# Padding the on-chip buffers of a softcap attention + MLP kernel so that matmul operands start at other addresses modulo 256

## The chip, the cores and the metric

The kernel runs on one core of a Trainium2 chip. The metric is the device time of one execution in microseconds (us); the median over the runs of a version counts. Matmuls run on TensorE (PE in the profile, its weight loads PEld), elementwise work on VectorE (DVE), ScalarE (ACT) and GpSimd (POOL), and transfers are issued mostly by SyncE (SP). SBUF is the on-chip memory of 128 partitions; an address below is the byte offset inside a partition.

## What is computed

Attention with a soft cap over 4 batches, 12 heads, 448 positions and head size 64, then a two-layer MLP on its 1792 x 768 result, all in float32:

```python
scores = cap * np.tanh(scale * (q @ k.T) / cap)
attn = np.exp(scores - scores.max(-1)); attn = attn / (attn.sum(-1) + 1e-09)
x = (attn @ v)                      # heads side by side: 1792 x 768
h = x @ w_in                        # 768 x 2048
g = np.maximum(0.01 * h, h)
return g @ w_out                    # 2048 x 768
```

## The kernel before

The 24 pairs of heads (4 batches, 6 pairs each) are worked on one after the other. For a pair, the transposed keys and queries lie in SBUF, `scores` (L490 to L499) multiplies them into PSUM, ScalarE applies tanh and exp (L521, L523) into the tiles `pf`, `values` (L504) multiplies `pf` with the rows of v, and VectorE divides by the sums and writes a piece of x. The first 12 pairs use full float32 matmuls; from pair 12 on (`fs=12`), keys and queries are split into a high and a low part of type float32r, and three products stand for one.

The MLP runs over four stretches of the 1792 rows. The first stretch (256 rows) multiplies float32 tiles: weights from `ws`, columns from `bank_0` and three later banks (L673). The second (512 rows) splits weights and columns into high and low parts of type float32r, so that each product is three matmuls of 128 x 128 weights and 512 moving columns: high x high, high x low, low x high (L673). The third and fourth stretch are done together in a scheme with seven products of sums and differences of blocks (`plan_duo`, L895), followed by the second layer (`plan_last`, L992), again three float32r matmuls of 512 columns per product.

All weights of the float32r matmuls of the MLP lie in the four tiles `w_0` to `w_3`. The moving columns lie in many places: in `xh` and `xl` (the parts of x for the second stretch), in the eleven `bank_j` tiles (parts of the hidden layer), and, once attention is over, in the memory that held `raws`, `odd`, `exps`, `norm` and `heads_h` during attention, which `places` hands out in slots of 512 columns. The list is

```python
homes = xl_slots + places("raws") + places("heads_h") + places("odd") + places("exps") + places("norm") + bank_slots
```

Every tile is made by `tile_of` (L210), directly, through `ring`, or through `chunk` (one tile that holds several small ones), in a pool with one buffer per name. The pool lays the tiles one behind the other in the order in which they are made and rounds each size up to a multiple of 32 bytes. `life` makes a second, third or fourth tile under the tag of an old one and so reuses its address. All columns that a matmul picks out of a tile start a multiple of 256 bytes behind the tile's start (512 float32 columns are 2048 bytes, 448 are 1792, 128 are 512, 64 are 256). So a tile's start modulo 256 is also the start modulo 256 of every operand read from it.

The order of the work is set by `Plan.issue`, a planner with costs and due times written into the table `T`; it knows nothing of addresses.

Of the kernel before, what the change touches and what calls it, by code (L numbers as in the profile page):

```python
# [9 lines left out]
F32 = mybir.dt.float32  # L10
# [151 lines left out]
def softcap_attention_mlp(  # L162
# [14 lines left out]
    P = 128  # L177
# [29 lines left out]
    def f32(ap):  # L207
        return ap.bitcast(F32)

    def tile_of(name, shape, dt=F32, pool=const, tag=None):  # L210
        t = pool.tile(shape, dt, name=name, tag=tag or name)
        return t

    def ring(tag, n, shape, dt=F32, pool=const):
        plan.ring(tag, n)
        tiles[tag] = [tile_of(f"{tag}_{i}", shape, dt, pool) for i in range(n)]
# [9 lines left out]
    def chunk(name, *parts):  # L226

        size = sum(n * cols for _, n, cols, _ in parts)
        whole = tile_of(name, [P, size])
        chunks[name] = (size, [])  # L230
        rows, lo = {}, 0
        for tag, n, cols, view in parts:
            for i in range(n):
                ap = whole[:, lo:lo + cols]
                lo += cols
                rows.setdefault(tag, []).append(ap.rearrange(view[0], **view[1]) if view else ap)
                chunks[name][1].append((tag, i))
        return rows
# [48 lines left out]
    for tag in ("kT", "qT"):  # L287
        alias(tag, rows[tag + "0"] + rows[tag + "1"], [0 if parted_of(i) else i % 2 for i in range(n_pairs)])
    heads_h = tile_of("heads_h", [P, 2, S], F32R)
    for x, nm in enumerate("kq"):  # L290
        alias(nm + "h", [heads_h[:, x]])
# [864 lines left out]
```

## Time and profile before

| | us |
|---|---|
| median of 3 runs | 688.72 |
| lowest and highest of them | 687.26, 2277.24 |
| profiled execution, whole | 689.4 |
| profiled execution, span from first to last instruction | 687.6 |
| PE busy in the span | 653.6 |

The durations below are those of the profiled execution; 1.8 us of it lie outside the span. In the profile a matmul's end is modelled and overlaps the next matmul's start, so what one costs in a dense stream is read from the distance between starts: the start of the next row of the timeline minus the start of this one, divided by the number of matmuls in this one. A full float32 matmul stands as two records, a float32r matmul as one.

### The profile page before, as it was taken

The page shows a single profiled execution, that of the slowest core. Times are in us where ns is not written, and L with a number is a line of the kernel's source. Part 1 is how long each engine was busy: PE and PEld are TensorE (multiplying, and loading weights), DVE is VectorE, ACT ScalarE, POOL GpSimd, SP SyncE. Part 2 cuts the span into 40 slices and gives each one's busy share as a digit, 9 for nine tenths or more (in the row PEclk, how much of TensorE's full clock was granted, in tenths as well). Part 3 has the DMA queues.
Part 4 walks back from the last instruction along what each step waited for, and adds up shares of the span by engine and source line. Part 5 has one row for each costly group of instructions (what it writes and reads, how often), then busy time and mean ns, then how long its engine had stood idle before and what let it go on. Part 6 is the DMA issues. An engine that isn't in the chain of part 4 may idle for free.

```text
span 687.6 us, 8588 instructions
## 1 busy us (share of the span) xinstructions
PE 653.6 (95%) x2932; PEld 457.7 (67%) x2932; DVE 446.9 (65%) x693; ACT 367.7 (53%) x611; POOL 73.5 (11%) x87
## 2 busy tenths in 40 slices
PE   8878989999989899999999999999999899999995
PEld 4223455566666567878666878878788687888884
DVE  3739759887889997587687786864856881121210
ACT  5877959886879776484575353433424840110000
POOL 8111201000121020010310020000000200000000
PEclk9998999999999999999999999999999999999999
DMA  9888988998859877312233143310212213144212
GB/s 135 138 237 166 260 246 197 303 256 259 232 130 227 229 170 198 115 46 85 74 91 91 58 95 86 84 47 23 82 33 57 91 42 73 38 92 92 38 27 33
DMA packets 186308, 85.60 MB, mean 124 GB/s; under 512 B 148240, under 2 KB 172816, under 8 KB 186256
## 3 DMA queue, kind: packets, MB, share of 16 engines
q1 hardware_dynamic: 182576, 83.23, 49.0%
q0 software_dynamic: 768, 1.38, 1.1%
q10 hardware_dynamic: 2912, 0.36, 0.4%
q8 instruction: 25, 0.41, 0.3%
q14 instruction: 27, 0.22, 0.1%
HBM read 66.85 MB, written 18.09 MB: 124 GB/s over the span
## 4 chain that ended last, share of the span: by engine, by line
PE 77%; DVE 8%; ACT 6%; DMA 6%; issue 1%; SPq 1%; DVEq 0%; ACTq 0%
PE m L673 27%; PE sc L992 19%; PE sc L895 11%; PE po L504 7%; PE po L895 4%; PE sc L493 3%; DMA bank<-in_moe_w_in_dram 3%; PE m L895 2%; ACT exps L521 2%; PE sc L499 2%; DVE bank L626 1%; DVE ws L629 1%; ACT exps L523 1%; PE sc L490 1%; DMA scratch<-ws 1%
## 5 line engine op out<-in xcount | busy, mean ns | idle before, releaser
L258 ACT CAST w<-ws 128x384 fp32r<-128x384 f32 (+2 forms) x99 | 62.9, 654 | 133.8 <-PE sc L992 75.1
L265 DVE TENSOR_TENSOR w<-ws,w 128x384 fp32r<-128x384 f32 (+2 forms) x93 | 68.0, 744 | 74.8 <-ACT w L258 74.4
L673 PE MATMUL m<-bank,ws 128*128 128x256 f32 x384 | 92.7, 391 | 2.8 <-DVE ws L629 2.8
L673 PEld LDWEIGHTS m<-bank,ws 128*128 128x128 f32 x384 | 71.7, 192 | 28.6 <-DVE ws L629 8.1
L521 ACT ACTIVATE exps<-sc 128x896 f32<-128x896 f32 (+1 forms) x96 | 76.0, 819 | 27.2 <-PE sc L493 15.1
L504 PE MATMUL po<-exps,norm 128*64 128x448 f32 x384 | 79.5, 547 | 1.3 <-ACT exps L523 0.7
L523 ACT ACTIVATE exps<-exps 128x896 f32<-128x896 f32 (+1 forms) x96 | 79.8, 857 | 0.4
L673 PE MATMUL m<-bank,w 128*128 128x512 f32 x288 | 68.5, 392 | 0.0
L992 PE MATMUL sc<-bank,w 128*128 128x512 f32 x270 | 64.2, 390 | 0.0
L673 PEld LDWEIGHTS m<-bank,w 128*128 128x128 f32 x288 | 53.5, 188 | 12.8 <-issue 1.3
L673 PE MATMUL m<-xh,w 128*128 128x512 f32 x192 | 61.4, 393 | 0.0
L992 PEld LDWEIGHTS sc<-bank,w 128*128 128x128 f32 x270 | 50.7, 188 | 10.9
L504 PEld LDWEIGHTS po<-exps,norm 128*64 128x64 f32 x384 | 25.0, 136 | 45.7 <-issue 36.8
L673 PEld LDWEIGHTS m<-xh,w 128*128 128x128 f32 x192 | 36.0, 188 | 9.7 <-DVE w L265 0.7
L1005 DVE STREAM_TRANSPOSE ot<-sc 128x512 f32<-128x512 f32 x12 | 8.6, 717 | 49.0 <-PE sc L992 49.0
L673 PE MATMUL m<-xl,w 128*128 128x512 f32 x96 | 37.4, 390 | 0.0
L622 ACT ACTIVATE bank<-bank 128x768 int32<-128x768 uint8 (+1 forms) x34 | 29.8, 875 | 12.2 <-DMA bank<-in_moe_w_in_dram 9.9
L626 DVE SCALAR_TENSOR_TENSOR bank<-bank 128x768 int32<-128x768 int32 (+1 forms) x34 | 30.9, 913 | 3.5 <-ACT ws L624 3.4
L527 DVE TENSOR_TENSOR norm<-exps 128x896 f32<-128x896 f32 x23 | 24.9, 1083 | 11.3 <-ACT exps L523 6.6
L629 DVE SCALAR_TENSOR_TENSOR ws<-ws,bank 128x768 int32<-128x768 int32 (+1 forms) x34 | 31.6, 930 | 0.5
L530 POOL TENSOR_TENSOR norm<-norm,exps 64x448 f32<-64x448 f32 x12 | 14.9, 1239 | 154.9 <-ACT exps L523 95.2
L624 ACT ACTIVATE ws<-bank 128x768 f32<-128x768 f32 (+1 forms) x34 | 29.6, 874 | 0.2
(188 smaller groups left out, 1056.2 us busy)
## 6 DMA issues: line engine op xcount, KB each, us to landing
ws<-scratch SPq DMA_DIRECT2D x44, 384.0 KB, 3.1
bank<-in_moe_w_in_dram SPq DMA_DIRECT2D x16, 768.0 KB, 6.2
scratch<-ws SPq DMA_DIRECT2D x22, 384.0 KB, 4.2
bank<-in_moe_w_out_dram SPq DMA_DIRECT2D x12, 640.0 KB, 5.4
ws<-scratch SPq DMA_DIRECT2D x24, 320.0 KB, 2.9
raws<-in_k_dram SPq DMA_DIRECT2D x96, 56.0 KB, 3.9
norm<-in_v_dram SPq DMA_DIRECT2D x48, 96.0 KB, 4.1
bank<-in_moe_w_out_dram SPq DMA_DIRECT2D x6, 768.0 KB, 6.5
```

The source lines that it names most:

```text
L258: nc.scalar.copy(o, i)
L265: ENG[eng].tensor_tensor(out=o, in0=a, in1=f32(b), op=ALU.subtract)
L504: nc.tensor.matmul(at("po", 2 * i)[half[j], 0:S], at("vc", i)[:, c], pf(g)[:, j if wide(g) == 2 else 0], start=(g == 0), stop=(g == NG - 1))
L521: a = plan.add(r, {"act": ct}, lambda e, sc=sc, g=g: nc.scalar.activation(pf(g), sc(), AF.Tanh, scale=scale_of["tanh"]), vers("sc", [g]) + ...
L523: plan.add(r, {"act": ct + 0.03}, lambda e, g=g: nc.scalar.activation(pf(g), pf(g), AF.Exp, scale=scale_of["exp"]), (), vers("pf", [g]), a ...
L622: a = plan.add(rank, {"act": ca}, lambda e: nc.scalar.activation(word(0), top(), AF.Copy, bias=1.0 / 64 - 0.5, scale=1.0 / 32), [("wr", m) ...
L624: b = plan.add(rank, {"act": ca}, lambda e: nc.scalar.activation(ws(), word(1).bitcast(F32), AF.Abs, scale=2.0 ** -112), [("wr", m)], [("w ...
L626: a = plan.add(rank, {"dve": cv}, lambda e: nc.vector.scalar_tensor_tensor(out=word(1), in0=word(1), scalar=-0x80000000, in1=word(0), op0= ...
L629: plan.add(rank, {"dve": cv}, lambda e: nc.vector.scalar_tensor_tensor(out=z(), in0=z(), scalar=3, in1=word(1), op0=ALU.logical_shift_left ...
L673: nc.tensor.matmul(ps(), l, r, start=begins and some[0] == 0 and i == 0, stop=ends and some[-1] == len(cs) - 1 and i == len(ops) - 1)
L895: nc.tensor.matmul(ps(), l, r, start=start and x == 0, stop=x == len(ops) - 1, skip_group_check=not start)
L992: nc.tensor.matmul(ps(), l, rr, start=first and x == 0, stop=final and x == len(ops) - 1)
```

## The change

`tile_of` gets a table of nine names. Ahead of a tile whose name is in it, it makes one more tile of 8 float32 (32 bytes) times the number in the table, which nothing reads or writes. All tiles made later move up by the same amount.

```diff
+    PADS = {"raws": 1, "odd": 1, "exps": 1, "norm": 1, "heads_h": 1, "xh": 5, "xl": 1, "bank_0": 1, "w_0": 7}
+
     def tile_of(name, shape, dt=F32, pool=const, tag=None):
+        if PADS.get(name):
+            pool.tile([P, 8 * PADS[name]], F32, name=f"pad_{name}", tag=f"pad_{name}")
         t = pool.tile(shape, dt, name=name, tag=tag or name)
         return t
```

No instruction is added, removed or moved: on every engine the built program has the same rows in the same order, with the same semaphores waited for; only buffer numbers and addresses differ. The pads are 19 times 32 bytes, 608 in all, and the last tile now ends at byte 228864 of its partition instead of 228256. The start addresses in the two built programs, modulo 256, and the number of float32r matmuls of 512 columns that read their moving columns there (1656 in all; their weights are in `w` each time):

```
tile            before          after    moving 512-column matmuls
raws        16928 =  32     16960 =  64      112
odd         27680 =  32     27744 =  96       42
exps        32288 =  32     32384 = 128      210
norm        53792 =  32     53920 = 160      210
heads_h     75808 =  32     75968 = 192       14
xh          80288 = 160     80608 = 224      192
xl          92576 = 160     92928 =   0      222
bank_0     118688 = 160    119072 =  32      654 (all banks; each is 6144 = 24 x 256 bytes)
ws_0       194464 = 160    194848 =  32        -
w_0        203680 = 160    204288 =   0        weights of all 1656
```

So in the kernel before, 1068 of these matmuls (`bank`, `xl`, `xh`) move columns from the same address modulo 256 as their weights, and 588 (`raws`, `odd`, `exps`, `norm`, `heads_h`) from an address 128 bytes away from it. In the changed kernel the distance is 32 bytes for `bank`, 32 on the other side for `xh`, 0 for `xl`, 64 for `raws`, 96 for `odd`, 128 for `exps`, 96 on the other side for `norm` and 64 on the other side for `heads_h`. The float32 matmuls of the first stretch (`bank_0` and `ws`) keep the distance 0.

## Rows read from the trace of the kernel before

**Rows 1.** The page, busy time, share of the span and instructions of each engine.
```profile
PE 653.6 (95%) x2932; PEld 457.7 (67%) x2932; DVE 446.9 (65%) x693; ACT 367.7 (53%) x611; POOL 73.5 (11%) x87
```
**Rows 2.** The page, chain that ended last, share of the span by engine.
```profile
PE 77%; DVE 8%; ACT 6%; DMA 6%; issue 1%; SPq 1%; DVEq 0%; ACTq 0%
```
**Rows 3.** Busy time of each engine in stretches of the span.
```profile
core 0: us, PE busy (x) PEld busy (x) DVE busy (x) ACT busy (x) POOL busy (x), PEclk, DMA share, GB/s
...
43.00:240.00 197.00, 185.42 (x852) 108.18 (x852) 162.09 (x251) 158.78 (x256) 23.85 (x28) 0.97 0.89 232
...
254.00:400.00 146.00, 145.75 (x692) 107.32 (x692) 109.28 (x153) 85.28 (x141) 14.33 (x9) 1.00 0.34 92
400.00:577.00 177.00, 172.33 (x741) 137.51 (x737) 120.46 (x199) 75.66 (x144) 13.34 (x10) 1.00 0.24 65
577.00:687.60 110.60, 101.85 (x443) 82.69 (x441) 18.00 (x23) 8.36 (x11) 0.00 (x0) 0.99 0.28 56
```
**Rows 4.** Waits of PE from 250 to 687 us, longest of seven and the shortest.
```profile
PE sc L895 <- ACT bank L258: 1.4, 2, 0.7
PE sc L895 <- DVE xh L905: 1.2, 1, 1.2
...
PE po L551 <- DVE xh L581: 0.2, 1, 0.2
```
**Rows 5.** Timeline of PE, 651 to 674 us: start, us, operation, count.
```profile
651.30 6.31 PE L992 MATMUL sc<-bank,w 128*128 128x512 f32 x27
657.44 2.20 PE L992 MATMUL sc<-xl,w 128*128 128x512 f32 x9
659.48 1.79 PE L992 MATMUL sc<-raws,w 128*128 128x512 f32 x7
661.11 0.39 PE L992 MATMUL sc<-heads_h,w 128*128 128x512 f32 x1
661.34 0.40 PE L992 MATMUL sc<-raws,w 128*128 128x512 f32 x1
661.58 1.56 PE L992 MATMUL sc<-norm,w 128*128 128x512 f32 x6
...
668.45 2.26 PE L992 MATMUL sc<-norm,w 128*128 128x512 f32 x9
670.55 0.86 PE L992 MATMUL sc<-odd,w 128*128 128x512 f32 x3
671.25 2.27 PE L992 MATMUL sc<-exps,w 128*128 128x512 f32 x9
673.35 0.85 PE L992 MATMUL sc<-bank,w 128*128 128x512 f32 x3
```
**Rows 6.** Chain that ended last, in order of time: start, us, what.
```profile
118.79 2.59 PE m L673 x12
123.99 2.79 PE m L673 x12
```
**Rows 7.** Timeline of PE in attention, float32r scores of a pair.
```profile
246.17 0.37 PE L493 MATMUL sc<-heads_h,odd 64*128 64x448 f32 x2
246.38 0.37 PE L493 MATMUL sc<-heads_h 64*128 64x448 f32 x2
246.58 0.37 PE L493 MATMUL sc<-odd,heads_h 64*128 64x448 f32 x2
246.79 0.37 PE L493 MATMUL sc<-heads_h,odd 64*128 64x448 f32 x2
```
**Rows 8.** Line L258 on ACT: duration ns min/median/max, by tiles.
```profile
L258 ACT CAST bank<-bank x7: 614/622/635, 544.1 to 552.1; 128x512 fp32r<-128x512 f32 x7
...
L258 ACT CAST norm<-bank x5: 621/622/625, 537.1 to 539.2; 128x512 fp32r<-128x512 f32 x5
```
**Rows 9.** Line L265 on DVE: duration ns min/median/max, by tiles.
```profile
L265 DVE TENSOR_TENSOR bank<-wait,bank x6: 684/689/691, 426.4 to 562.8; 128x512 fp32r<-128x512 f32 x6
...
L265 DVE TENSOR_TENSOR exps<-bank,exps x5: 685/687/687, 550.6 to 560.4; 128x512 fp32r<-128x512 f32 x5
```
**Rows 10.** Issues of DMA: count, KB each, median us to landing.
```profile
raws<-in_k_dram SPq DMA_DIRECT2D x96, 56.0 KB, 3.9
```

## The prediction

> **What bounds the kernel now.** I read the page's busy shares first: TensorE is busy for 95% of the span [rows 1], and 77% of the chain that ended last is PE [rows 2]. A busy share of PE says little by itself, so the stretches come next [rows 3]. From 254 us on, PE is busy for 145.75 of 146, 172.33 of 177 and 101.85 of 110.6 us, while DVE and ACT have room (120.46 and 75.66 of 177) and the DMA engines are at 0.24 to 0.34. In these 433 us stand all 1656 float32r matmuls of 512 columns. The waits of PE from 250 us on come to under 6 us: seven rows, the longest 1.4 us [rows 4]. So there the time is the number of matmuls times the distance between their starts, and what a pad does to that distance goes into the end nearly one for one. Before 240 us attention and the first stretch of the MLP share the chip: PE 185.42 of 197 us, with ACT, DVE and DMA nearly as full [rows 3].
>
> The timeline then gives that distance by the tile that the columns come from [rows 5]. Nine matmuls on `xl` start at 657.44 and the next row at 659.48: 2.04 / 9 = 0.2267 us each. Twenty-seven on `bank`: (657.44 - 651.30) / 27 = 0.2274. The nine on `raws` and `heads_h` from 659.48 to 661.58: 0.2333; nine on `norm`, 668.45 to 670.55: 0.2333; nine on `exps`, 671.25 to 673.35: 0.2333. Same shape, same weight tiles, same stage, no wait between. What differs is the address: `xl` and `bank` start at 160 modulo 256 like their weights, the other four at 32, 128 bytes away. So start addresses cost 0.0067 us per matmul, and this trace has two points of the curve.
>
> A third row I take as the floor: twelve records of the float32 matmuls of 256 columns take 2.59 us, 0.2158 each [rows 6] (the 2.79 us run beside it begins after another kind of matmul). A record there has half the columns and takes nearly as long, so it must spend about twice the time on a column and need its operands at about half the rate. So 0.0109 us of the 0.2267 and 0.0175 of the 0.2333 lie above the floor, and reading operands out of SBUF is the likeliest owner.
>
> The Trainium skill, page "SBUF — State Buffer", section "Who interferes with whom", says that PE's read port for moving columns and its port for weights are independent and that PE never waits on anyone. By that the pads change nothing. The 0.2267 against 0.2333 speaks against it; it is a rival below.
>
> **The change part by part.** Nothing is added or moved on any engine, and no wait is new; the one thing to price is the distance between starts of each group of matmuls. I take the reading that the surcharge follows the distance between the moving columns and the weights modulo 256, since both streams are read at the same time. Known are distance 0 (0.2267) and 128 (0.2333). Distances 32, 64 and 96 are not in this trace. Their lower bound is the floor, 0.2158. Their upper bound is 0.24: the largest single distance in the rows, from 661.34 to 661.58, and as far above 0.2333 as that lies above 0.2267. Between ends this far apart I take 0.2300, midway between the two rows measured on this shape, because nothing says which of the two an in-between distance resembles.
>
> - `bank`, 654 matmuls, distance 0 to 32: 654 x (0.2300 - 0.2267) = +2.2 us.
> - `xh`, 192, distance 0 to 32 on the other side: +0.6 us.
> - `raws`, `odd`, `norm`, `heads_h`, together 378, distance 128 to 64 or 96: 378 x (0.2300 - 0.2333) = -1.2 us.
> - `xl`, 222, stays at 0 and `exps`, 210, at 128: nothing. Cover for that is the reading itself; under the second rival below they do change.
> - Scores of the last 12 pairs: each pair has 12 starts of 448 float32r columns about 0.207 us apart [rows 7]. In 8 of the 12 columns and weights now lie in `heads_h` and `odd`, 96 apart, where both stood at 32. 96 x 0.0033 x 448/512 = +0.3 us; bounds are -1.0 and +1.1 by the same two ends.
> - Float32 matmuls: `bank_0` with `ws` keeps distance 0. `values` goes from 0 to 32 (columns in `exps`, weights in `norm`). They need their operands at the half rate of the floor row [rows 6], so 0. If that cover were gone, 192 starts x 0.0067 = 1.3 us, in a stage where PE has 11.6 us of idle time in 197 to soak it up [rows 3]; and no less than 0, as they have nothing to lose.
> - ACT and DVE: the same cast takes 622 ns with its output at 160 or at 32 modulo 256 [rows 8], the two-input subtraction 689 and 687 [rows 9]. Priced at 0, bounded by those 2 ns x 700 instructions, 1.4 us to either side, beside other work.
> - DMA: every start stays a multiple of 32 bytes; only `raws` now begins on one of 64. Its 56 KB pieces land in 3.9 us [rows 10] and are issued pairs ahead. Priced at 0. Were they a tenth faster or slower, one first load, 0.4 us, would show at the start.
>
> Sum: 2.2 + 0.6 - 1.2 + 0.3 = +1.9 us on the profiled execution's 689.4, so 691.3. That execution is 0.7 above the median of the runs shown, 688.72; against that the forecast is 690.6. The bounds: at the floor all 1656 give 1068 x 0.0109 + 588 x 0.0175 = 21.9 us less, 667 against the median; at 0.24 the changed groups give 846 x 0.0133 + 378 x 0.0067 + 1.1 = 14.9 us more, 703.6.
>
> The Trainium skill, page "TensorE: Matmul & The Clock Gate", section "Back-to-back issue gap", gives a spacing of N / 2.4 + 2.5 ns for an isolated matmul, 215.8 ns at 512 columns. The floor above agrees (0.2158), the float32r rows do not; by the rule alone there would be 21.9 us to win, the low bound just given.
>
> **Rivals.**
>
> *Addresses do nothing.* The difference between the tiles would come from something that goes with them and not from their place. For it: both groups vary by some ns. Against it: six groups of tiles, split exactly by address, with the same weights. Time 688.7.
>
> *The moving address alone counts, not the weights'.* Then `bank` takes over the row of address 32: 654 x 0.0067 = +4.4. `norm` arrives at 160: 210 x -0.0067 = -1.4. `xl` and `xh`, 414, go to unknown addresses, midway: +1.4; `exps`, `raws`, `odd`, `heads_h`, 378, likewise: -1.2. Sum +3.2, so 691.9. For it: in this trace all weights of these matmuls sit at 160, so the two readings can't be told apart; the scores with both operands at 32 are about 0.207 apart, 0.018 above the floor of 0.2158 x 448/512 = 0.189, where distance 0 would give 0.0109 x 448/512 = 0.010 and address 32 would give 0.015. Against it: these come in short runs of pairs, and the first matmuls of a run are slower anyway.
>
> *Faster: the half-line rule.* All operands before start 32 bytes past a multiple of 64. If the surcharge is that of reading across such a border, then `xl`, `exps`, `raws` and `heads_h`, now with their weights on multiples of 64, fall to the floor: 222 x 0.0109 + 336 x 0.0175 = 8.3 us, so 680.4. If the weights' alignment alone decides, all 1656 do, 667. For it: the surcharge exists at distance 0 too. Against it: 32 and 160 are alike in this respect and yet cost different amounts, so it can't be the whole.
>
> *Slower: the two streams run into each other at 32 bytes.* Place: `bank` and `xh`, 846 matmuls, half of the whole. The two streams start a few ns apart, and a neighbour on either side could be met at each step where an equal start is met at few. A spacing of 0.2500, the same 0.0233 above 0.2267 that is a tenth of the matmul, costs 846 x 0.0233 = 19.7 us: 708.4. It decides from 0.2430 up, where 846 x 0.0163 = 13.8 us is 2% of the time. For it: most matmuls are moved from the cheapest distance known. Against it: 128 bytes away, the farthest from equal, costs just 0.0067.
>
> **How the numbers follow.** Forecast with its prices between the two rows: 0.55. Moving address alone: 0.20. Half-line rule for the four groups: 0.09; for all by the weights: 0.03. Streams that collide: 0.07. Nothing: 0.06. The likeliest case gives 690.6. The range 681 to 700 holds the forecast with `bank` and `xh` anywhere from 0.2187 (846 x 0.0080 = 6.8 us less, and 0.9 for the other terms) up to their bound of 0.24 (699.1), the second rival and no change; outside stay the half-line cases (0.12) and the collision (0.07). About 2% is what a measurement of this kernel can tell from no change, 13.8 us. Over 2% faster: the all-weights case and a little of the forecast's lower tail, 0.04. Over 2% slower: the collision and a little of the upper tail, 0.08. Within: 0.88.
>
> **What would show it right or wrong.** In the timeline of the changed kernel the runs on `xl` should again be 0.2267 apart and those on `exps` 0.2333 if distance counts; if the moving address alone counts, `norm` shows 0.2267 and `bank` 0.2333. `bank` is the row to read first: each 0.001 us on it is 0.65 us of the whole. The float32 runs should stay at 0.2158, the casts at 622 ns, and the waits of PE after 250 us under 6 us. The prediction is wrong if `bank` leaves 0.2187 to 0.24, or if the time moves while these distances do not.

## The result, and the profile after

The changed kernel takes 693.05 us (median of 6 runs, 689.97 to 694.52), the kernel before 688.11 (6 runs beside it): a ratio of 1.0069 with a 95% interval of 1.0041 to 1.0096. It is slower, by about 4.9 us, and by less than 2%. One of the six executions of the kernel before took 2277.24 us; the ratio leaves it out, and the median without it is 687.50. The profiled execution spans 690.9 us against 687.6.

The split of the span at the 1004th matmul record, which is the same place in both programs, says where. The first view is busy time by stretches of the kernel before, the second of the changed kernel.

```profile
0.00:243.00 243.00, 222.69 (x1004) 123.10 (x1004) 189.33 (x302) 190.20 (x305) 41.23 (x63) 0.98 0.89 215
243.00:687.60 444.60, 430.93 (x1931) 334.57 (x1928) 257.60 (x392) 177.53 (x307) 32.26 (x24) 1.00 0.30 75
```
```profile
0.00:242.00 242.00, 219.99 (x1004) 121.78 (x1004) 189.53 (x302) 190.32 (x305) 41.74 (x64) 1.00 0.89 216
242.00:690.90 448.90, 435.72 (x1930) 334.56 (x1928) 257.74 (x392) 177.39 (x307) 32.31 (x24) 0.99 0.29 74
```

The part with the float32r matmuls grew from 444.6 to 448.9 us, 4.3 more, and PE's busy time with it (4.8). DVE, ACT and POOL are busy as long as before. The clock is not the difference: from 240 to 680 us the granted clock is 1.00 in every stretch of 20 us of both traces. The first part is 1.0 us shorter in this pair of executions. Nothing should be read into that: in the five experiments below that have every tile of attention at 160, the 1005th matmul record starts anywhere between 241.5 and 243.4 us.

The timeline of PE in the changed kernel, for the same stretch as [rows 5] (start, us, operation, count; the distance between starts is the next row's start minus this one's, over the count):

```profile
654.43 6.46 PE L996 MATMUL sc<-bank,w 128*128 128x512 f32 x27
660.73 2.23 PE L996 MATMUL sc<-xl,w 128*128 128x512 f32 x9
662.79 1.78 PE L996 MATMUL sc<-raws,w 128*128 128x512 f32 x7
664.41 0.39 PE L996 MATMUL sc<-heads_h,w 128*128 128x512 f32 x1
664.64 0.40 PE L996 MATMUL sc<-raws,w 128*128 128x512 f32 x1
664.88 1.57 PE L996 MATMUL sc<-norm,w 128*128 128x512 f32 x6
...
671.89 2.25 PE L996 MATMUL sc<-norm,w 128*128 128x512 f32 x9
673.98 0.86 PE L996 MATMUL sc<-odd,w 128*128 128x512 f32 x3
674.68 2.26 PE L996 MATMUL sc<-exps,w 128*128 128x512 f32 x9
676.78 0.40 PE L996 MATMUL sc<-bank,w 128*128 128x512 f32 x1
```

`bank` went from 0.2274 to 6.30 / 27 = 0.2333. `xl` went from 0.2267 to 0.2289, `raws` with `heads_h` from 0.2333 to 0.2322, `norm` from 0.2333 to 0.2322; `exps` stayed at 0.2333. The starts are printed to 0.01 us, so over nine matmuls 0.0011 is one step of the print. The merged chain shows the same over longer stretches, here its rows of 108 matmuls on `xh` and `xl` and of the last 441, before and after:

```profile
267.19 24.70 PE m L673 x108
...
578.07 101.59 PE sc L992 x441
```
```profile
266.34 25.15 PE m L677 x108
...
580.28 102.97 PE sc L996 x441
```

0.2287 became 0.2329 on `xh` and `xl`, and 0.2304 became 0.2335 at the end. What the pads do not touch stayed: a run of twelve float32 records of 256 columns still takes 2.59 us, as in [rows 6], and the casts below still take 618 and 620 ns at the median ([rows 8]: 622 for both).

```profile
117.77 2.59 PE m L677 x12
```
```profile
L262 ACT CAST bank<-bank x7: 613/618/624, 546.0 to 554.1; 128x512 fp32r<-128x512 f32 x7
...
L262 ACT CAST norm<-bank x5: 620/620/623, 539.1 to 541.2; 128x512 fp32r<-128x512 f32 x5
```

### The profile page after: what moved, and what is told of

Same layout as the page of the kernel before. It is cut to its first block, busy times and chain, and to the rows that moved or that the text cites. A ratio compares the mean times of both kernels' runs of the same rounds, so it can differ in the third digit from the quotient of the medians.

```text
span 690.9 us, 8588 instructions
## 1 busy us (share of the span) xinstructions
PE 655.7 (95%) x2932; PEld 456.3 (66%) x2932; DVE 447.3 (65%) x693; ACT 367.7 (53%) x611; POOL 74.0 (11%) x87
## 4 chain that ended last, share of the span: by engine, by line
PE 79%; DMA 7%; DVE 6%; ACT 5%; issue 1%; SPq 1%; DVEq 0%; ACTq 0%
PE m L677 27%; PE sc L996 19%; PE sc L899 11%; PE po L508 8%; PE po L899 4%; DMA bank<-in_moe_w_in_dram 3%; PE sc L497 3%; PE m L899 2%; PE sc L503 2%; DMA raws<-in_k_dram 2%; ACT exps L525 1%; DVE bank L630 1%; PE sc L494 1%; ACT exps L527 1%; DVE ws L633 1%
## 5 line engine op out<-in xcount | busy, mean ns | idle before, releaser
L677 PE MATMUL m<-bank,w 128*128 128x512 f32 x288 | 70.0, 397 | 0.0
L996 PE MATMUL sc<-bank,w 128*128 128x512 f32 x270 | 65.7, 395 | 0.0
```

Of the source, the lines that this page charges most:

```text
L677: nc.tensor.matmul(ps(), l, r, start=begins and some[0] == 0 and i == 0, stop=ends and some[-1] == len(cs) - 1 and i == len(ops) - 1)
L996: nc.tensor.matmul(ps(), l, rr, start=first and x == 0, stop=final and x == len(ops) - 1)
```

## Experiments

The theory: the distance between starts of float32r matmuls of 512 columns follows the moving address minus the weight address, modulo 256; in the trace of the kernel before, a weight load starts 2 to 4 ns after nearly every one of these matmuls, so both are read at the same time. Rivals: the moving address alone counts; operands off a multiple of 64 pay. All kernels below differ from the changed one in the table alone. A distance is the moving address minus the weight address, modulo 256.

**Weights moved alone.** All moving columns stay where they were before, the weights go from 160 to 32.

```diff
-    PADS = {"raws": 1, "odd": 1, "exps": 1, "norm": 1, "heads_h": 1, "xh": 5, "xl": 1, "bank_0": 1, "w_0": 7}
+    PADS = {"w_0": 4}
```

> Only the four weight tiles move, by 128 bytes, to 32 modulo 256; every moving address stays as before. Distance theory (the surcharge follows moving address minus weight address modulo 256): the two groups trade places, bank, xl and xh (1068 matmuls) go from 0.2267 to 0.2333 us and the 588 others from 0.2333 to 0.2267; 1068 x 0.0066 - 588 x 0.0066 = +3.2 us, 691.3 against 688.1. Rival, the moving address alone counts: bank stays at 0.227, norm and exps at 0.233, 688.1. Half-line rival (all still 32 past a multiple of 64): no change either.

Measured 689.76 us against 688.45, ratio 1.0024 (1.0004 to 1.0043). Its timeline:

```profile
653.83 6.42 PE L996 MATMUL sc<-bank,w 128*128 128x512 f32 x27
660.09 2.26 PE L996 MATMUL sc<-xl,w 128*128 128x512 f32 x9
662.19 1.77 PE L996 MATMUL sc<-raws,w 128*128 128x512 f32 x7
...
673.93 2.20 PE L996 MATMUL sc<-exps,w 128*128 128x512 f32 x9
675.97 6.46 PE L996 MATMUL sc<-bank,w 128*128 128x512 f32 x27
```

The groups traded places without having moved: `xl` 2.10 / 9 = 0.2333 where it was 0.2267, `exps` 2.04 / 9 = 0.2267 where it was 0.2333, `bank` 6.26 / 27 = 0.2319 where it was 0.2274. This ends the rival of the moving address alone, and the one by which addresses do nothing. The loss in time, 1.3 us, is smaller than the 3.2 expected: `bank` pays 0.0045 here, not 0.0066. Over all starts of these matmuls in the trace that follow one another within 0.3 us, the mean goes from 0.2296 to 0.2310, which is 2.3 us for 1656 and lies inside the interval (0.3 to 3.0 us).

The single starts of the two traces also show that a group does not take its own distance at once. In the kernel before, the first five matmuls of a run on `bank` after the second stretch are 0.2291 to 0.2329 apart on average, and 0.2267 from the ninth on; with the weights moved, the first five of a run on `exps` are 0.2277 to 0.2311 apart and the later ones 0.2268 to 0.2276. With every matmul at distance 0 the runs have no such beginning. So a run of nine behind a run at another distance is a mixture, and the kernels below, with one distance for all, are the ones to read the levels from.

**Distance 0 for all.** Moving columns and weights all at 160.

```diff
-    PADS = {"raws": 1, "odd": 1, "exps": 1, "norm": 1, "heads_h": 1, "xh": 5, "xl": 1, "bank_0": 1, "w_0": 7}
+    PADS = {"raws": 4, "xh": 4}
```

> Moving columns of every group and the weights at 160 modulo 256: distance 0 for all 1656. Distance theory: the 588 matmuls on raws, odd, exps, norm and heads_h fall from 0.2333 to 0.2267, 588 x 0.0066 = 3.9 us less, 684.2, below both kernels. Moving address alone: the same, as 160 is its cheap address. Half-line rival: 688.1, nothing moves against a multiple of 64.

Measured 683.73 against 688.45, ratio 0.9943 (0.9919 to 0.9967): faster than both kernels, by the size expected. In its chain the last 441 matmuls take 100.27 us, 0.2274 each, where the kernel before took 101.59.

```profile
575.50 100.27 PE sc L996 x441
```

**Distance 32 for all.** As the last one, with the weights at 128.

```diff
-    PADS = {"raws": 4, "xh": 4}
+    PADS = {"raws": 4, "xh": 4, "w_0": 7}
```

> As the kernel with distance 0 for all, but the weights at 128: every moving column 32 bytes ahead of its weights. Distance theory, with the 0.2333 that bank shows at 32 in the changed kernel: all 1656 at 0.2333, 1656 x 0.0066 = 10.9 us above the kernel with distance 0, so 695.1. Moving address alone: 684.2, since all stay at 160. Half-line rival: weights now on a multiple of 64, so not slower than 688.1.

Measured 693.12, ratio 1.0077 (1.0050 to 1.0103), 9.4 us above the kernel with distance 0 (expected 10.9). Its timeline has 0.2333 for `bank` (6.30 / 27) as for `xl` (2.10 / 9):

```profile
654.73 6.47 PE L996 MATMUL sc<-bank,w 128*128 128x512 f32 x27
661.03 2.26 PE L996 MATMUL sc<-xl,w 128*128 128x512 f32 x9
663.13 1.80 PE L996 MATMUL sc<-raws,w 128*128 128x512 f32 x7
```

So 32 bytes cost as much as 128, and do so with the moving columns at 160, the address at which they were cheapest before.

**Distances 64, 96 and 192 for all.** As above with the weights at 96, 64 and 224; one execution each.

```diff
-    PADS = {"raws": 4, "xh": 4, "w_0": 7}
+    PADS = {"raws": 4, "xh": 4, "w_0": 6}   # 5 for distance 96, 2 for distance 192
```

> All moving columns at 160, weights at 96: distance 64. In the changed kernel the runs on raws (distance 64) were mixed, about 0.229 to 0.231 after neighbours at other distances. Distance theory with a smooth rise from 0 to 32 and a plateau: about 0.233. Distance theory with 64-byte pieces (only a distance that is no multiple of 64 costs the full step): 0.2290, 1656 x 0.0023 = 3.8 us above the kernel with distance 0 for all, 687.5.

> Distance 96. Smooth theory and piece theory alike: 0.2335, 1656 x 0.0068 = 11.3 us above the kernel with distance 0 for all, 695.

> Distance 192, 64 bytes behind the weights. Piece theory: 0.2310 (what heads_h showed) or the 0.2290 of distance 64, if the sign does not count; 687.5 to 690.8. Smooth theory: 0.233 and 694.

Single times: 687.87, 693.40 and 693.96 us. The timelines, in this order:

```profile
656.37 2.22 PE L996 MATMUL sc<-xl,w 128*128 128x512 f32 x9
658.43 1.77 PE L996 MATMUL sc<-raws,w 128*128 128x512 f32 x7
```
```profile
655.04 6.46 PE L996 MATMUL sc<-bank,w 128*128 128x512 f32 x27
661.34 2.26 PE L996 MATMUL sc<-xl,w 128*128 128x512 f32 x9
```
```profile
655.38 6.46 PE L996 MATMUL sc<-bank,w 128*128 128x512 f32 x27
661.68 2.26 PE L996 MATMUL sc<-xl,w 128*128 128x512 f32 x9
```

Distance 64 costs 0.2289, between the two levels; 96 and 192 cost 0.2333. Neither of my two forms of the theory holds whole. The smooth one is refuted by 64, which is cheaper than 32. The one with pieces of 64 bytes is refuted by 192 and 128, multiples of 64 that pay in full. The curve as measured with all matmuls at one distance: 0: 0.2267, 32: 0.2333, 64: 0.2289, 96: 0.2333, 192: 0.2333; 128, in the kernel before and with the weights moved: 0.2333. Each level is that of one profiled execution; over all starts in these traces the means are 0.2271, 0.2333, 0.2291, 0.2334 and 0.2333.

**All at 0 modulo 256.** Distance 0, on a multiple of 64.

```diff
-    PADS = {"raws": 4, "xh": 4}
+    PADS = {"raws": 7, "xh": 4}
```

> All operands of the float32r matmuls at 0 modulo 256: distance 0 again, but on a multiple of 64 (and of 256). Distance theory: 684.2 and 0.2267 everywhere, as with all at 160. Half-line rival: 0.2158 everywhere, 667. Moving address alone: open, 0 is neither of the two addresses of before; xl lies there in the changed kernel at about 0.230, which would give 1656 x 0.230 against 1656 x 0.2267, 5.5 us above the kernel with all at 160.

Measured 679.89, ratio 0.9881 (0.9855 to 0.9907): the fastest of all. But not through the matmuls, which keep the distance they have with everything at 160; the last 441 take 100.27 us again:

```profile
570.38 100.27 PE sc L996 x441
```

The half-line rival falls: its 0.2158 was not reached. What was gained lies before: the 1005th matmul record starts at 238.2 us, against 241.5 to 243.4 in the kernels with all tiles of attention at 160. The issues of DMA of the kernel with all at 160 and of this one (count, KB each, median us from issue to landing):

```profile
raws<-in_k_dram SPq DMA_DIRECT2D x96, 56.0 KB, 4.0
norm<-in_v_dram SPq DMA_DIRECT2D x48, 96.0 KB, 4.0
...
raws<-in_q_dram POOLq DMA_DIRECT2D x24, 56.0 KB, 4.6
```
```profile
raws<-in_k_dram SPq DMA_DIRECT2D x96, 56.0 KB, 2.7
norm<-in_v_dram SPq DMA_DIRECT2D x48, 96.0 KB, 3.0
...
raws<-in_q_dram POOLq DMA_DIRECT2D x24, 56.0 KB, 2.8
```

and their first 43 us (busy time by engine; the last two numbers are the mean busy share of the DMA engines and GB/s):

```profile
0.00:43.00 43.00, 35.59 (x136) 13.89 (x136) 24.68 (x47) 31.22 (x49) 17.32 (x35) 0.96 0.91 144
```
```profile
0.00:43.00 43.00, 35.97 (x150) 15.70 (x152) 26.52 (x51) 34.11 (x54) 18.19 (x36) 1.00 0.76 162
```

More bytes moved at a smaller busy share, and 150 matmuls done instead of 136. Three more kernels ask which transfers gain.

**All at 128; `raws` alone at 0; `norm` alone at 0.** The last two leave everything else at 160.

```diff
-    PADS = {"raws": 7, "xh": 4}
+    PADS = {"raws": 3, "xh": 4}                              # all at 128
+    PADS = {"raws": 7, "odd": 5, "xh": 4}                    # raws alone at 0
+    PADS = {"raws": 4, "norm": 3, "heads_h": 5, "xh": 4}     # norm alone at 0
```

> All operands at 128 modulo 256, distance 0: spacing 0.2267 by the distance theory, as at 160 and at 0. The 3.8 us by which all at 0 beat all at 160 arose before 240 us, where loads of k, q and v landed in 2.7 to 3.0 us instead of 4.0. If transfers pay for pieces that straddle a multiple of 256, the 128-byte pieces of raws straddle none at 128 (half of them do at 160) and land in 2.7 us, while the 256-byte rows of v all straddle one and stay at 4.0: about 681. If they pay for straddling a multiple of 128, both are as fast as at 0: 680. If only a start at 0 counts, 683.7.

> As all at 160, but raws alone (the tiles that k and q land in) at 0. If the loads of k and q carry the gain of all at 0, they land in 2.7 us and the time falls by most of 3.8 us, less 112 matmuls at distance 96, +0.7: about 681. If the loads of v carry it, 684.4 and no change in the landing of k.

> As all at 160, but norm alone (the tile that v lands in) at 0. If the loads of v carry the gain, they land in 3.0 us and the time falls by most of 3.8 us, less 210 matmuls at distance 96, +1.4: about 681.5. If the loads of k and q carry it, 685 with v still near 4 us.

Measured 682.74 (0.9919, 0.9894 to 0.9944), 682.21 (0.9912, 0.9884 to 0.9940) and 685.39 (0.9949, 0.9929 to 0.9969). Landings, in this order:

```profile
raws<-in_k_dram SPq DMA_DIRECT2D x96, 56.0 KB, 2.9
norm<-in_v_dram SPq DMA_DIRECT2D x48, 96.0 KB, 3.3
```
```profile
raws<-in_k_dram SPq DMA_DIRECT2D x96, 56.0 KB, 2.9
norm<-in_v_dram SPq DMA_DIRECT2D x48, 96.0 KB, 3.4
```
```profile
raws<-in_k_dram SPq DMA_DIRECT2D x96, 56.0 KB, 3.6
norm<-in_v_dram SPq DMA_DIRECT2D x48, 96.0 KB, 3.7
```

`raws` at 0 or at 128 brings k down to 2.9, and v, issued on the same queue, to 3.3 and 3.4. To read the rest one has to know how far executions differ. Five kernels above have `raws` and `norm` at 160 and differ in the weights alone: k lands there in 4.0, 3.6, 4.0, 4.2 and 3.9 us (distance 0, 32, 64, 96, 192), v in 3.7 to 4.0. Here k at distance 32 and 96:

```profile
raws<-in_k_dram SPq DMA_DIRECT2D x96, 56.0 KB, 3.6
```
```profile
raws<-in_k_dram SPq DMA_DIRECT2D x96, 56.0 KB, 4.2
```

So the 3.6 and 3.7 with `norm` at 0 show no gain, and the 3.6 in the changed kernel, with `raws` at 64, shows none either; 2.7 to 2.9 lie well outside. The loads of q on the POOL queue divide in the same way: 2.8 to 2.9 with `raws` at 0 or 128, 4.2 to 4.7 with it at 32, 64 or 160. The first 43 us agree, here with `raws` alone and with `norm` alone at 0:

```profile
0.00:43.00 43.00, 36.48 (x144) 16.28 (x144) 26.40 (x50) 33.30 (x53) 17.68 (x36) 0.98 0.76 156
```
```profile
0.00:43.00 43.00, 35.18 (x136) 14.51 (x136) 24.97 (x47) 31.01 (x49) 17.32 (x35) 0.98 0.88 144
```

With `raws` at 0 or 128 the DMA engines are at 0.76 and 144 to 150 matmuls are done; in the nine other kernels they are at 0.88 to 0.92 and 136 to 138 are done. So the place of `raws` sets how fast its own loads of k and q land. What that is worth in time is less sure. `raws` alone takes 1.5 us less than all at 160 by the medians, 2.2 with the 0.7 us added back that its 112 matmuls at distance 96 cost, of the 3.8 us that all at 0 takes less. But the intervals of all at 160, of `raws` alone and of all at 128 overlap, and so do those of `raws` alone and all at 0, so neither the share of `raws` nor that of the other tiles is settled. The time with `norm` at 0 is that of all at 160 plus the 1.4 us for 210 matmuls at distance 96.

The Trainium skill, page "DMA: Bandwidth & Descriptors", section "How a descriptor splits into AXI transactions", tells of reads that they go in pieces starting at multiples of 256 bytes. The landings of k and q fit such a rule on the SBUF side: 128-byte pieces from 0 or 128 on stay inside one, and from 32, 64 or 160 on every second straddles two. Pieces of 128 bytes would fit these rows as well. The 256-byte rows of v do not show it: none straddles with `norm` at 0, all do at 160, and 3.7 is still within what 160 gives.

## Why the prediction was right, and where it was off

The forecast was 690.6 us, a little slower and within 2%; measured were 693.05 and +0.7%. The way to it held: the time followed the distance between starts of the float32r matmuls, and this followed moving minus weight address, which was argued from two distances and is now shown by the kernel that moves the weights alone. The size was 1.9 us where 4.9 came. That the sign came out right was in part luck: it hung on the midway price. With the in-between distances as cheap as 0 the same sum gives 378 x -0.0066 = -2.5 us, with all of them as dear as 128 it gives 846 x 0.0066 + 96 x 0.0066 x 448/512 = +6.1. By its own terms:

- `bank`, from distance 0 to 32, was taken midway at 0.2300. This is the step that failed: it measured 0.2333, so that the 654 matmuls cost 654 x (0.2333 - 0.2274) = 3.9 us, not 2.2. The argument "nothing says which of the two an in-between distance resembles" was fair; the answer is that 32 costs as much as 128.
- `xh`, likewise, and `xl`, priced at nothing: on the second stretch, where the two alternate, 288 matmuls went from 0.2287 to 0.2329 (the rows of 108), +1.2 us instead of 0.6. The other 126 on `xl` went from 0.2267 to 0.2289, +0.3, although their own distance is 0 before and after, so what the prediction named as a mark of being right, 0.2267 again on `xl`, did not come. Their neighbours slow them: in the run of nine shown above, the single starts are 230, 236, 228, 232 and 231 ns apart and then 227, 227, 226 and 227, and with every matmul at distance 0 the same run is at 226 or 227 throughout.
- `raws`, `odd`, `norm` and `heads_h` were to give 1.2 us back. At 0.2322 they would give 378 x 0.0011 = 0.4, one step of the print. Over all their starts in the two traces `raws` went from 0.2332 to 0.2312, but `odd` from 0.2326 to 0.2337 and `norm` from 0.2330 to 0.2339: together they gave nothing back.
- `exps` stayed at 0.2333, as said. These terms make 3.9 + 1.2 + 0.3 - 0.4 = 5.0. The mean over all starts, 0.2296 before and 0.2326 after, gives 1656 x 0.0030 = 5.0 as well. The part after the 1004th record grew by 4.3.
- The scores in attention, +0.3, are lost in the differences between executions. Float32 matmuls, ACT and DVE at 0: right (2.59 us a run, 618 to 620 ns a cast).
- DMA at 0 was right for this change: 3.9 us before and 3.6 after are both within the 3.6 to 4.2 that kernels with `raws` at one address show. The bound beside it, 0.4 us, was far too narrow: `raws` at 0 shows landings in 2.9 us, and all at 0 takes 3.8 us less than all at 160. The step that misled was to price the first load alone, where the DMA engines are at 0.89 until 240 us [rows 3].

Of the rivals, the moving address alone would have given `bank` the very 0.2333 that it shows, and a time of 691.9, closer than the forecast. It is still wrong: `norm`, moved to 160, stands at 0.2322 and not at 0.2267, and with the weights moved alone the groups trade places. The half-line rule is refuted by all at 0. A collision at 32 bytes is not seen: 32 costs 0.2333, as 96, 128 and 192 do, and not 0.2500. That addresses do nothing is refuted by the kernel with the weights moved alone. The Trainium skill, page "SBUF — State Buffer", section "Who interferes with whom", calls PE's two read ports independent; here the distance between starts depends on both addresses together (0.2267 against 0.2333), so they do not behave as independent.

The floor of the prediction, 0.2158, comes from float32 records of 256 columns and is no measure of a float32r matmul of 512: the lowest level that any kernel here shows for these is 0.2267.

Three things stay open: how the two reads come to depend on each other, which no run shows; what makes 64 cheaper than 192; and what the 0.0109 us are that remain above the float32 row at distance 0.

## What to carry to other kernels

Lay the weights and the moving columns of float32r matmuls at the same address modulo 256: 1656 matmuls of 512 columns at distance 0 instead of 32 took 9.4 us less, and pads that spread the addresses made a kernel slower in which most were equal by luck. Lay tiles that receive transfers in 128-byte pieces at a multiple of 128 where the DMA engines are busy. All tiles at 0 modulo 256, which is both together, by two pads, took 1.2% off this kernel. When a profile shows one operation with one shape at two speeds, sort its rows by the address of each operand before looking for a wait, and read the levels from long runs: here the first five or so matmuls behind another group still carried that group's beat.

## Hardware behaviour that I had not expected

The surcharge is no smooth function of the distance: 0.2267 at 0, 0.2333 at 32, 0.2289 at 64, 0.2333 at 96, 128 and 192. The landing of a 56 KB load of 128-byte pieces depends on where in SBUF it lands: 2.7 to 2.9 us at 0 or 128 modulo 256, 3.6 to 4.2 at 32, 64 or 160. A float32r matmul behind a group at another distance does not run at its own level at once: runs on `bank` at distance 0 of the kernel before reached 0.2267 only after some five to seven matmuls (0.2291 to 0.2329 until then).
